# One more transposing transfer, three more masks by ScalarE's copy and a new order in a kernel of attention and feed-forward

## The chip, the cores and the metric

The kernel runs on one core of one Trainium2 chip. A core has five engines: TensorE (PE in the profile, with PEld for its weight loads), VectorE (DVE), ScalarE (ACT), GpSimd (POOL) and SyncE (SP). The metric is device microseconds of one execution. Each text below speaks of "steps" by the names that the kernel gives them.

## The reference

The input is r, k, v, w of shape (4, 8, 768, 48) (batch, heads, time, width), u of shape (8, 48), and four matrices. First comes a recurrence over time for each batch and head, then a feed-forward block on the 3072 tokens.

```
for t in range(S):
    cur = einsum('bhd,bhe->bhde', u * k[t], v[t])
    y[t] = einsum('bhd,bhde->bhe', r[t], state + cur)
    state = w[t][..., None] * state + einsum('bhd,bhe->bhde', k[t], v[t])
x = y transposed and reshaped to (3072, 384)
out = ((x @ w1) * (x @ w2)) @ w3 @ w_out      # 384 -> 1024 -> 1024 -> 384
```

## The kernel before

Time is cut into six chunks of 128 steps. The work is 13 **units**: a unit is one chunk c of one or two batches (`UNITS[t] = (c, b0, nb)`). Units 0 and 1 are the first chunk of batches 0 and 1 alone; every other unit has two batches. The recurrence inside a chunk becomes matrix products, and the state goes from chunk to chunk.

For each unit t there are these steps:

- **Loads:** win, kin, rin, vin (w, k, r, v), each as one DMA from the queue that the order names.
- **Decay:** ln (logarithm of w, ACT), cs or csT (cumulated sum, PE), ne, e, et, iw, pc (exponentials, ACT).
- **Scaled k and r:** KRk, rw, KRr or KRw (multiplies), then their transposes, by PE (trk, trr, trw with the evictions trke, trre) or by a transposing transfer on SP (dtk, dtr).
- **Diagonal term:** rk, ruk, dg, dv: r times k, times u, summed over the width (L530), times v (L539).
- **Scores:** m_t_b (PE, L551), then the mask. There are two ways. `msk` is one DVE multiply from PSUM (L570). For the pairs (t, b) in POOL_MASK it is `mcp`, a copy to SBUF by ACT (L557), and then `maff` on that copy in SBUF: a DVE multiply by the mask (L563) or a POOL select (L565).
- **y:** ys (state part, L586) and yi (scores by v, L596) add up in PSUM. Then `yb` adds dv on DVE (L614). For the units in Y_PE, `yd` adds dv by two PE matmuls with the identity (L605) and `ybc` copies (L611).
- **Transpose of y:** for the units in DMA_Y two transposing transfers on SP, `dty_t_b` (L623); for others `yt` (PE transposes, L633) and `xT` (copy, L637).
- **State:** kv (PE, L667), T (L674), S (times the decay, L689), Sb (copy to bf16).
- **Feed-forward:** a_t_g and b_t_g (PE, L714: x by w1 and by w2, in groups g of 512 columns), asb (copy of a, L719), abT (DVE product of a and b, L724), o_t_b (PE, L730, by the product w34 of w3 and w_out), osb (copy, L735), st (store on SP, L740).

The product w34 is made once, in eight blocks wt, w3Te, wm (L380), w34e. `uc` and `vc_0` cast u and unit 0's v. `warmB@N` runs N matmuls of zeros into PSUM bank B (L308).

What sets the order is a list written out as text, `ORDER`: each entry is `step@engine`, and the program calls the steps in this list's order. Each engine takes its own instructions in that order, and waits in it. `BANKS` gives every step its PSUM bank and its buffers. Between engines only data and buffers order the work. The loads from POOL's queue and POOL's arithmetic stand in one line; the same holds for the transfers and stores on SP.

```
for e in ORDER.split():
    name, _, eng = e.partition("@")
    if name.startswith("warm"):
        warm(int(name[4:]), int(eng))
        continue
    steps[name](eng)
```

Of the kernel before, what the change touches and what calls it, by code (L numbers as in the profile page):

```python
# [62 lines left out]
table@ACT zeros@DVE padlw@DVE win_0@POOL ones@DVE LT@POOL ln_0@ACT warm0@17 cs_0@PE ne_0@ACT win_1@POOL win_2@POOL
kin_2@POOL padkr@DVE csT_0@PE rin_0@SP padr@DVE I128@POOL rin_2@POOL rin_1@POOL rc_0@ACT trw_0@PE et_0@ACT kin_0@SP
kc_0@DVE KRk_0@DVE ln_1@ACT mask1@DVE warm7@2 csT_1@PE pc_0@ACT rk_0@DVE cs_1@PE ne_1@ACT padet@DVE KRw_0@DVE ln_2@ACT
pc_1@ACT trk_0@PE trke_0@DVE kin_1@POOL warm7@2 m_0_0@PE u@SP csT_2@PE cs_2@PE w3_0@POOL vin_0@SP vc_0@DVE kv_0@PE
mcp_0_0@ACT ne_2@ACT uc@DVE ruk_0@DVE dg_0@DVE S_0@DVE rk_2@DVE mask@POOL vin_2@POOL w2_0@POOL KRk_2@DVE trw_2@PE
et_2@ACT dv_0@DVE KRw_2@DVE trk_2@PE trke_2@ACT KRk_1@DVE warm7@5 m_2_0@PE maff_0_0@DVE yi_0_0@PE yd_0@PE ruk_2@DVE
wt_0_0@PE wt_0_1@PE dg_2@DVE et_1@ACT wt_1_0@PE pc_2@ACT mcp_2_0@ACT maff_2_0@DVE trk_1@PE trke_1@DVE w1_1@POOL
vin_1@POOL m_2_1@PE trw_1@PE w2_1@POOL w1_0@POOL kv_2@PE wt_1_1@PE w3Te_0@ACT ybc_0@ACT w3Te_1@ACT win_3@POOL yt_0@PE  # L70
msk_2_1@DVE yi_2_0@PE yi_2_1@PE dv_2@POOL yd_2@PE ybc_2@ACT KRw_1@DVE m_1_0@PE xT_0@DVE rk_1@DVE wo@POOL ruk_1@POOL
# [718 lines left out]
```

## Time and profile before

| | before |
|---|---|
| median of 3 runs | 164.85 us (164.43 to 165.8) |
| the profiled execution: its time | 164.84 us |
| the profiled execution: its span (first to last instruction) | 163.1 us |
| granted TensorE clock | 1.00 |
| PE busy | 154.6 us, 1922 matmuls |
| PE weight loads | 117.4 us |
| DVE busy | 125.2 us, 202 instructions |
| ACT busy | 100.5 us, 166 instructions |
| POOL busy | 97.8 us, 90 instructions |

How to read the rows of the profile: a row of a timeline has start, duration, engine, line of the kernel, operation, output and inputs with their shape, the count of instructions merged in it, and in brackets the idle time before it with what ended that. A row of the windows has, for a stretch of the span, its length, then busy time and count of PE, PEld, DVE, ACT and POOL, the granted clock, the share of the DMA engines and GB/s. A row of the groups has busy time and mean duration in ns, then the idle time in front and what ended it. Rows of the chain of waits have start, duration and what was waited for. Ends of matmuls are modelled and overlap; their starts are recorded.

### The profile page before, as it was taken

The numbers are of one execution on the slowest core, as the hardware profiler recorded it, in microseconds if no ns is written. First come the engines' busy times: TensorE is split into PE (matmuls) and PEld (weight loads), VectorE is DVE, ScalarE is ACT, GpSimd is POOL, SyncE is SP. The second block draws the span as 40 slices with busy tenths as digits, with TensorE's granted clock in tenths as the row PEclk, the third lists the DMA queues.
The fourth block names the chain that finished last, engine by engine and source line by source line (L and its number), as shares of the span: only waits on it lengthen the run. The fifth ranks groups of instructions, "written<-read, shape, count | busy, mean of one in ns | idle before, by whom it ended". The sixth has DMA issues, their size and how long they took to land.

```text
span 163.1 us, 4587 instructions
## 1 busy us (share of the span) xinstructions
PE 154.6 (95%) x1922; PEld 117.4 (72%) x1922; DVE 125.2 (77%) x202; ACT 100.5 (62%) x166; POOL 97.8 (60%) x90
## 2 busy tenths in 40 slices
...
GB/s 119 216 154 184 195 193 244 207 171 212 238 153 174 164 216 244 124 113 83 148 225 99 175 188 147 169 171 144 186 162 158 158 170 95 87 55 45 55 147 96
DMA packets 98837, 25.63 MB, mean 157 GB/s; under 512 B 90880, under 2 KB 96640, under 8 KB 98816
## 3 DMA queue, kind: packets, MB, share of 16 engines
...
## 4 chain that ended last, share of the span: by engine, by line
PE 65%; DVE 14%; DMA 13%; issue 3%; POOL 2%; ACT 1%; DVEq 0%; POOLq 0%; ACTq 0%
PE banks L714 25%; PE banks L730 16%; DMA wo_bf<-in_moe_w_out_dram 8%; PE banks L380 7%; DMA win<-in_w_dram 5%; PE banks L551 3%; DVE dv L539 3%; DVE yb L614 2%; PE banks L371 2%; PE banks L596 2%; DVE abT L724 2%; PE banks L424 2%; PE banks L512 2%; PE banks L667 2%; DVE Mbf L570 1%
## 5 line engine op out<-in xcount | busy, mean ns | idle before, releaser
L714 PE MATMUL banks<-xT,w_bf 128*128 128x256 bf16 (+1 forms) x624 | 69.2, 264 | 0.7 <-DVE yb L614 0.4
L714 PEld LDWEIGHTS <-w_bf 128*128 128x128 bf16 x624 | 55.3, 98 | 8.2 <-issue 1.0
L719 ACT COPY a_sb<-banks 128x512 f32<-128x512 f32 x48 | 27.9, 589 | 25.8 <-PE banks L714 19.0
L724 DVE TENSOR_TENSOR abT<-a_sb,banks 128x512 bf16<-128x512 f32 x48 | 31.6, 682 | 14.9 <-ACT a_sb L719 7.9
L730 PE MATMUL banks<-w,abT 128*128 128x384 bf16 x192 | 33.8, 326 | 0.0
L730 PEld LDWEIGHTS <-abT 128*128 128x128 bf16 x192 | 18.2, 98 | 10.9
L570 DVE TENSOR_TENSOR Mbf<-banks,mask 128x1024 bf16<-128x1024 f32 x15 | 18.1, 1220 | 2.1 <-PE banks L551 2.1
L335 POOL DMA_DIRECT2D win<-in_w_dram x13 | 14.8, 1143 | 5.3 <-ACT NEt L441 3.2
L735 ACT COPY osb<-banks 128x384 f32<-128x384 f32 x21 | 10.0, 482 | 12.8 <-PE banks L730 12.8
L408 ACT ACTIVATE lw<-win 128x768 bf16<-128x768 f32 (+1 forms) x13 | 10.4, 796 | 8.5 <-DMA win<-in_w_dram 8.5
L530 DVE TENSOR_REDUCE dg<-ruk 128x16 f32<-128x768 bf16 (+1 forms) x13 | 11.5, 886 | 0.8 <-POOL ruk L524 0.7
L565 POOL TENSOR_SCALAR_AFFINE_SELECT Mbf<-Mbf 128x1024 bf16<-128x1024 bf16 x5 | 5.5, 1090 | 11.0 <-ACT Mbf L557 11.0
L380 PE MATMUL banks<-wo_bf,w3T 128*128 128x384 bf16 x64 | 11.6, 326 | 0.1
L335 POOL DMA_DIRECT2D kin<-in_k_dram x8 | 9.1, 1133 | 4.1 <-DMA win<-in_w_dram 2.8
L614 DVE TENSOR_TENSOR yb<-banks,dv 128x768 bf16<-128x768 f32 (+1 forms) x11 | 10.1, 919 | 1.8 <-PE banks L596 1.3
L441 ACT ACTIVATE NEt<-banks 128x768 bf16<-128x768 f32 (+1 forms) x13 | 9.9, 764 | 1.5 <-PE banks L424 1.1
L308 PE MATMUL banks<-zeros 128*128 128x512 bf16 x28 | 9.4, 488 | 1.3 <-DVE zeros L249 1.3
L335 POOL DMA_DIRECT2D rin<-in_r_dram x8 | 9.0, 1124 | 2.1 <-DMA w_bf<-in_moe_w_dram 1.5
L557 ACT CAST Mbf<-banks 128x1024 bf16<-128x1024 f32 x9 | 9.0, 1011 | 0.6 <-PE banks L551 0.5
L335 POOL DMA_DIRECT2D vin<-in_v_dram x8 | 9.2, 1148 | 0.2
L524 POOL TENSOR_TENSOR ruk<-rk,u_bc 128x768 bf16<-128x768 bf16 (+1 forms) x4 | 5.8, 1450 | 5.7 <-DVE rk L520 5.7
L380 PEld LDWEIGHTS <-w3T 128*128 128x128 bf16 x64 | 5.8, 98 | 3.6 <-DMA wo_bf<-in_moe_w_out_dram 0.2
(100 smaller groups left out, 244.9 us busy)
## 6 DMA issues: line engine op xcount, KB each, us to landing
...
wo_bf<-in_moe_w_out_dram POOLq DMA_DIRECT2D x1, 768.0 KB, 13.1
```

What stands on the lines that cost most here:

```text
L335: QUEUE[eng].dma_start(dst, src)
L380: nc.tensor.matmul(one(f"wm{fi}")[:, :DM], lhsT=w3T[fi % 2][:, gi, :], rhs=wo_bf[:, gi, :], start=(gi == 0), stop=(gi == FI - 1))
L408: nc.scalar.activation(LW[:, :, :D], ww, Act.Ln)
L441: nc.scalar.activation(N_.rearrange("t (b h) d -> t b (h d)", b=nb), cs_view(), Act.Exp, scale=-1.0)
L530: nc.vector.reduce_sum(dgs, ruks, axis=AX.X)
L570: nc.vector.tensor_mul(Mbf[bank[f"M{t}_{b}"]], mview(), mask.rearrange("s (j q) t -> s j q t", j=2))
L614: nc.vector.tensor_add(ybs.rearrange("t b (q e d) -> t e (b q) d", e=2, d=D), yview().rearrange("t e (x d) -> t e x d", d=D), dvs.rearrang ...
L714: nc.tensor.matmul(o[:, f, :], lhsT=wt[:, di, fi * P:(fi + 1) * P], rhs=x[:, di, :T], start=(di == 0), stop=(di == DI - 1))
L719: copier(eng)(a_sb[bank[f"sa{t}_{g}"]], one(f"a{t}_{g}"))
L724: nc.vector.tensor_mul(ab[:, g * per:(g + 1) * per, :T], sa.rearrange("p (f t) -> p f t", t=T), one(f"b{t}_{g}").rearrange("p (f t) -> p f ...
L730: nc.tensor.matmul(one(f"o{t}_{b}")[:, :DM], lhsT=ab[:, fi, b * C:(b + 1) * C], rhs=w34[:, fi, :], start=(fi == 0), stop=(fi == FI - 1))
L735: copier(eng)(osb[bank[f"so{t}_{b}"]], one(f"o{t}_{b}")[:, :DM])
```

## The change

Three tables of settings change, and the two texts BANKS and ORDER are replaced as a whole. The functions stay as they are.

```diff
-DMA_Y = {4, 9, 10, 11, 12}
+DMA_Y = {4, 6, 9, 10, 11, 12}
-POOL_MASK = {(0, 0), (2, 0), (5, 0), (6, 1), (7, 1), (9, 0), (10, 0), (11, 1), (12, 1)}
-Y_PE = {0, 2}
+POOL_MASK = {(0, 0), (2, 0), (3, 0), (5, 0), (6, 1), (7, 1), (9, 0), (10, 0), (10, 1), (11, 0), (11, 1), (12, 1)}
+Y_PE = {0}
```

- Unit 6's y is transposed by two transfers on SP (dty_6_0, dty_6_1) in place of yt_6 (PE) and xT_6 (DVE).
- The masks (3,0), (10,1) and (11,0) are done by copy and maff in place of msk.
- Unit 2's dv is added by yb_2 on DVE in place of yd_2 (PE) and ybc_2 (ACT).
- win_9 and win_12 are issued by SP in place of POOL: win_9 after dty_4_1 and before dtr_7, win_12 after dtr_8.
- Steps that change engine: from DVE to POOL KRk_11, S_8, dv_11, maff_2_0, maff_12_1, rk_1, ruk_7, ruk_11, rw_8, uc, vc_0; from POOL to DVE KRk_8, KRr_8, maff_6_1, maff_10_0, rk_12, ruk_1, ruk_8, rw_11; from ACT to DVE osb_3_1, 4_0, 5_0, 6_0, 8_1, 11_0, 11_1, trke_3, 4, 5, Sb_6, rc_0, w34e_1, w34e_5, w3Te_1; from DVE to ACT osb_4_1, Sb_0, xT_0, w34e_0, w3Te_2, w3Te_4. New: maff_3_0 and maff_10_1 on DVE, maff_11_0 on POOL.
- The matmuls of zeros at the start: 17, 2, 2, 5, 2 before; 17, 5, 2, 3, 2, 3 after.

The order around the places that the text below speaks of, cut from the list:

```diff
 # before: the start, up to the first feed-forward block of unit 0
-... w3_0@POOL ... mask@POOL vin_2@POOL w2_0@POOL ... KRw_2@DVE ... w1_1@POOL vin_1@POOL ... w2_1@POOL w1_0@POOL ...
-... win_3@POOL yt_0@PE msk_2_1@DVE yi_2_0@PE yi_2_1@PE dv_2@POOL yd_2@PE ybc_2@ACT KRw_1@DVE m_1_0@PE xT_0@DVE rk_1@DVE wo@POOL
-ruk_1@POOL b_0_0@PE yt_2@PE warm5@2 a_0_1@PE ...
 # after
+... uc@POOL w3_0@POOL ... vin_2@POOL vin_0@SP vc_0@POOL ... mask@POOL w2_0@POOL ... w1_1@POOL ... w2_1@POOL vin_1@POOL ...
+... KRw_2@DVE ... w1_0@POOL ... maff_2_0@POOL ... KRk_1@DVE ... dv_0@DVE ... rk_2@DVE ruk_2@DVE dg_2@DVE ... trke_1@DVE ...
+... msk_2_1@DVE KRw_1@DVE ... S_2@DVE yi_2_0@PE yi_2_1@PE m_1_0@PE dv_2@POOL yb_2@DVE ... b_0_0@PE yt_2@PE ... warm7@3
+a_0_1@PE ... win_3@POOL b_2_0@PE wo@POOL rk_1@POOL ...
 # before: units 6 to 8
-... KRr_7@DVE dtr_7@SP S_6@DVE ne_8@ACT xT_5@ACT KRk_8@POOL ... yb_6@DVE ... yt_6@PE ... rw_8@DVE KRr_8@POOL ...
 # after
+... yb_6@DVE ... dty_6_0@SP a_5_0@PE ruk_7@POOL rin_9@POOL ... T_7@DVE ... S_6@DVE trk_7@PE rw_8@POOL KRr_8@DVE ... S_7@POOL ...
+... cs_10@PE ... dtk_8@SP rin_10@POOL dtr_8@SP b_6_0@PE win_12@SP ... KRk_9@POOL ... S_8@POOL ... rw_9@DVE KRr_9@POOL ...
 # after: unit 10
+... ruk_11@POOL ... KRk_11@POOL dtk_11@SP m_10_1@PE ys_10@PE m_10_0@PE dg_10@DVE mcp_10_1@ACT maff_10_1@DVE mcp_10_0@ACT KRr_11@DVE
+dtr_11@SP maff_10_0@DVE kv_10@PE KRk_12@DVE ... rw_12@DVE KRr_12@POOL ...
 # before: units 11 and 12
-... dg_11@DVE dv_11@DVE ... yb_11@DVE ... maff_12_1@DVE ... S_10@POOL ... msk_12_0@DVE rk_12@POOL ruk_12@DVE ...
 # after
+... maff_11_1@POOL ... dg_11@DVE ... maff_11_0@POOL ... S_9@POOL ys_11@PE dv_11@POOL S_10@POOL yi_11_0@PE yi_11_1@PE o_9_0@PE
+yb_11@DVE ... maff_12_1@POOL ...
```

More of the change, by code (lines that the diff above doesn't have):

```diff
@@ L61 @@
 """
 ORDER = """
[L63 to L71, printed above, removed]
-b_0_0@PE yt_2@PE warm5@2 a_0_1@PE asb_0_1@ACT msk_1_0@DVE xT_2@DVE b_2_0@PE S_2@DVE yi_1_0@PE a_2_2@PE dg_1@DVE
@@ L98 @@
-abT_4_2@DVE rw_8@DVE KRr_8@POOL trke_7@ACT ruk_7@DVE Sb_6@ACT kv_7@PE kv_8@PE T_8@DVE xT_6@DVE Sb_5@ACT T_7@DVE
-b_5_0@PE abT_5_0@DVE a_5_2@PE asb_5_3@ACT asb_5_2@ACT b_5_2@PE abT_5_2@DVE o_4_0@PE m_7_0@PE S_8@DVE ys_7@PE rk_8@DVE
-asb_5_1@ACT m_7_1@PE msk_7_0@DVE o_4_1@PE b_5_1@PE ln_9@ACT ruk_8@POOL dg_8@DVE osb_4_0@ACT st_4_0@SP ln_10@ACT
-mcp_7_1@ACT maff_7_1@POOL iw_9@ACT a_6_1@PE asb_6_1@ACT abT_5_1@DVE cs_10@PE ne_10@ACT e_10@ACT S_7@POOL dg_7@DVE
-osb_4_1@DVE st_2_0@SP b_6_1@PE dtr_8@SP pc_10@ACT b_6_2@PE b_5_3@PE win_12@POOL a_6_2@PE yi_7_0@PE yi_7_1@PE
@@ L128 @@
-osb_11_1@ACT st_11_1@SP o_11_0@PE osb_11_0@ACT abT_12_2@DVE st_11_0@SP abT_12_0@DVE abT_12_1@DVE o_12_0@PE o_12_1@PE
-osb_12_0@ACT o_10_1@PE st_12_0@SP osb_12_1@ACT st_12_1@SP osb_10_1@ACT st_10_1@SP
+table@ACT zeros@DVE ones@DVE padet@DVE kin_0@SP win_0@POOL ln_0@ACT LT@POOL padr@DVE padkr@DVE win_1@POOL win_2@POOL
+kin_2@POOL I128@POOL kc_0@DVE padlw@DVE warm0@17 cs_0@PE csT_0@PE et_0@ACT rin_0@SP rin_2@POOL rc_0@DVE trw_0@PE
+KRw_0@DVE ne_0@ACT KRk_0@DVE warm6@5 trk_0@PE ln_1@ACT kin_1@POOL rin_1@POOL ln_2@ACT u@SP uc@POOL w3_0@POOL rk_0@DVE
@@ new lines @@
+ruk_0@DVE trke_0@DVE warm0@2 m_0_0@PE mcp_0_0@ACT dg_0@DVE warm3@3 cs_2@PE cs_1@PE vin_2@POOL vin_0@SP vc_0@POOL
+pc_0@ACT kv_0@PE csT_2@PE mask1@DVE S_0@DVE trw_2@PE mask@POOL w2_0@POOL ne_2@ACT w1_1@POOL KRk_2@DVE trk_2@PE
+w2_1@POOL vin_1@POOL maff_0_0@DVE et_2@ACT KRw_2@DVE trw_1@PE ne_1@ACT w1_0@POOL pc_2@ACT trke_2@ACT warm7@2 m_2_0@PE
+yi_0_0@PE mcp_2_0@ACT maff_2_0@POOL KRk_1@DVE csT_1@PE et_1@ACT dv_0@DVE trk_1@PE yd_0@PE rk_2@DVE ruk_2@DVE dg_2@DVE
+wt_0_0@PE wt_0_1@PE trke_1@DVE pc_1@ACT ybc_0@ACT m_2_1@PE w3Te_0@ACT kv_2@PE yt_0@PE msk_2_1@DVE KRw_1@DVE wt_1_0@PE
@@ new lines @@
+S_2@DVE yi_2_0@PE yi_2_1@PE m_1_0@PE dv_2@POOL yb_2@DVE wt_1_1@PE xT_0@ACT b_0_0@PE yt_2@PE w3Te_1@DVE warm7@3
+a_0_1@PE xT_2@DVE b_2_1@PE a_2_3@PE a_2_2@PE asb_2_2@ACT msk_1_0@DVE asb_2_3@ACT win_3@POOL b_2_0@PE wo@POOL rk_1@POOL
+ruk_1@DVE dg_1@DVE dv_1@DVE yi_1_0@PE yb_1@DVE b_2_3@PE abT_2_3@DVE b_2_2@PE abT_2_2@DVE asb_0_1@ACT ln_3@ACT b_0_1@PE
+abT_0_1@DVE a_0_0@PE asb_0_0@ACT yt_1@PE xT_1@DVE a_2_0@PE kv_1@PE asb_2_0@ACT S_1@DVE Sb_1@DVE abT_0_0@DVE a_1_1@PE
+asb_1_1@ACT abT_2_0@DVE b_1_1@PE csT_3@PE et_3@ACT a_2_1@PE asb_2_1@ACT b_1_0@PE a_1_0@PE cs_3@PE abT_1_1@DVE ne_3@ACT
```

146 lines of the change are left out of this document (75 added, 71 removed).

## Prediction, made before the result was known

> **What bounds the kernel now.** I read the page first, then the busy time by stages, then the timelines of single engines where a stage shows TensorE idle.
>
> ```profile
> span 163.1 us, 4587 instructions
> ...
> PE 154.6 (95%) x1922; PEld 117.4 (72%) x1922; DVE 125.2 (77%) x202; ACT 100.5 (62%) x166; POOL 97.8 (60%) x90
> ```
>
> TensorE (PE) is busy 95% of the span, and the next engine, VectorE (DVE), 77%. The windows below cut the span where PE's behaviour changes; the first figure of a row is the length of the window, the second PE's busy time, and DVE is the third engine figure.
>
> ```profile
> 0.00:23.00 23.00, 18.99 (x204) 10.81 (x205) 15.89 (x41) 13.45 (x21) 19.95 (x27) 1.00 1.45 175
> 23.00:79.00 56.00, 55.94 (x777) 44.34 (x775) 46.41 (x74) 40.14 (x66) 38.22 (x33) 1.00 1.78 183
> 79.00:84.30 5.30, 4.82 (x82) 4.01 (x81) 5.30 (x8) 4.24 (x8) 4.66 (x5) 1.00 1.04 174
> 84.30:133.00 48.70, 48.70 (x634) 37.97 (x631) 42.57 (x62) 32.19 (x54) 35.02 (x28) 1.00 1.63 158
> 133.00:141.00 8.00, 7.78 (x100) 6.33 (x97) 7.45 (x9) 2.99 (x7) 0.00 (x0) 1.00 0.63 120
> ```
>
> From 23 to 141 us PE idles in two places only, 79 to 84.3 and 133 to 141, and in the first of them DVE is busy without a break (5.30 of 5.30). The granted clock is 1.00 throughout. So time can come from three sources: less PE work, an earlier start of the dense part at 23 us, and those two gaps. Because matmul ends are modelled, I measure the gaps from start to start.
>
> ```profile
> 79.80 1.47 PE L714 MATMUL banks<-xT,w_bf 128*128 128x256 bf16 x12
> 81.64 0.81 PE L714 MATMUL banks<-xT,w_bf 128*128 128x256 bf16 x6 [0.37 <-DVE yb L614]
> 82.29 0.50 PE L633 MATMUL banks<-I,yb 128*128 128x128 bf16 x6
> 82.91 0.81 PE L714 MATMUL banks<-xT,w_bf 128*128 128x256 bf16 x6
> ...
> 132.17 0.36 PE L586 MATMUL banks<-Sbf,KRT 64*128 64x48 bf16 x16
> 132.38 0.38 PE L551 MATMUL banks<-KRT 64*128 64x128 bf16 x8
> ...
> 134.51 0.37 PE L586 MATMUL banks<-Sbf,KRT 64*128 64x48 bf16 x16
> 135.03 2.78 PE L714 MATMUL banks<-xT,w_bf 128*128 128x256 bf16 x24
> ...
> 138.05 9.57 PE L714 MATMUL banks<-xT,w_bf 128*128 128x256 bf16 x84
> 147.46 0.81 PE L730 MATMUL banks<-w,abT 128*128 128x384 bf16 x4
> ```
>
> Six matmuls of L714 run from 81.64 to 82.29, 0.65 us. Twelve therefore need 1.30 us, but from 79.80 it took 1.84 until the next: 0.54 lost. The six transposes at 82.29 need 0.33 (half as many columns) and took 0.62: 0.29 lost. At 134.51 the sixteen L586 matmuls took 0.52 where those at 132.17 took 0.21: 0.31 lost. The 84 matmuls from 138.05 took 9.41 where 14 times 0.65 is 9.10: 0.31 lost. Together 1.45 us, in two places. Why DVE is late there stands in four rows of DVE and two of POOL (GpSimd):
>
> ```profile
> 77.31 0.55 DVE L689 TENSOR_TENSOR Sst<-Tst,pc 128x384 f32<-128x384 f32 x1
> ...
> 78.25 2.00 DVE L689 TENSOR_TENSOR Sst<-Tst,pc 128x384 f32<-128x384 f32 x1
> ...
> 130.78 3.05 DVE L539 TENSOR_TENSOR dv<-wo_bf,dg 128x768 bf16<-128x768 bf16 x1
> ...
> 138.19 0.96 DVE L539 TENSOR_TENSOR dv<-vin,dg 128x768 bf16<-128x768 bf16 x1
> ...
> 78.08 1.76 POOL L445 TENSOR_TENSOR KR<-w_bf,NEt 128x768 bf16<-128x768 bf16 x1 [1.91 <-ACT NEt L441]
> ...
> 131.37 1.63 POOL L520 TENSOR_TENSOR rk<-rin,kin 128x768 bf16<-128x768 bf16 x1
> ```
>
> The same state multiply (S, L689) takes 0.55 and 2.00 us, the same dv multiply (L539) 0.96 and 3.05. Each long one ends shortly after a POOL multiply that overlaps it: 80.25 against 78.08 + 1.76 = 79.84, and 133.83 against 131.37 + 1.63 = 133.00. So a DVE multiply of two operands in SBUF waits until POOL's is done, 1.45 and 2.09 us here, and everything behind it on DVE waits too: the yb (L614) that feeds PE at 81.64 is named in PE's own row. The Trainium skill, page "SBUF — State Buffer", section "Who interferes with whom", states this as a lock: a VectorE instruction with two SBUF inputs and a GpSimd instruction that reads SBUF exclude each other for a whole instruction. The two rows agree.
>
> **The change part by part.** *The transfer for y of unit 6* removes yt_6, six PE transposes, 0.33 us of PE, and xT_6, a DVE copy. It adds two transposing transfers on SyncE (SP).
>
> ```profile
> L623 SPq DMA_TRANSPOSE xT<-yb x10: 1177/1242/1312, 62.6 to 142.1; - x10
> ...
> DMA to landing us min/median/max: 2.3/4.0/6.7
> ...
> 80.64 0.94 DVE L614 TENSOR_TENSOR yb<-banks,dv 128x768 bf16<-128x768 f32 x1
> ...
> 91.18 0.33 PE banks L424 x2
> ```
>
> yb_6 ends at 81.6 (80.64 + 0.94). The second transfer is issued one issue (1.3) later and lands after 2.3 to 6.7 us: at 89.6 at worst. Its first reader, b_6_0, stands in the new order right behind cs_10, which is the row at 91.18 and ends at 91.5: a cover of 1.9 us even then. Cost nothing; without that cover, what is missing of it. The transposes go from PE: -0.33.
>
> *y of unit 2 on DVE* removes yd_2 (two PE matmuls) and an ACT copy and adds a yb on DVE, 0.96 us. This lies in the start, which is counted as a whole below.
>
> *Loads of w of units 9 and 12 by SP* take two issues from POOL. On SP they stand in front of dtr_7 and of stores; SP waits long there anyway:
>
> ```profile
> SPq L491 <- DVE KR L486: 13.1, 1, 13.1
> ```
>
> That is SP's wait for KRr_7 before dtr_7, 13.1 us, so an issue ahead of it (some 1.2 to 1.3 us by the transfers above) is hidden, as long as KRr_7 doesn't come over 10 us earlier. Both loads have a buffer whose last reader is long done. Nothing.
>
> *Three more masks by ACT's copy* (units 3, 10, 11).
>
> ```profile
> L570 DVE TENSOR_TENSOR Mbf<-banks,mask x15: 1214/1218/1225, 19.2 to 135.5; 128x1024 bf16<-128x1024 f32 x15
> ...
> L557 ACT CAST Mbf<-banks 128x1024 bf16<-128x1024 f32 x9 | 9.0, 1011 | 0.6 <-PE banks L551 0.5
> ...
> L563 DVE TENSOR_TENSOR Mbf<-Mbf,mask 128x1024 bf16<-128x1024 bf16 x4 | 2.7, 682 | 0.0
> ...
> L565 POOL TENSOR_SCALAR_AFFINE_SELECT Mbf<-Mbf 128x1024 bf16<-128x1024 bf16 x5 | 5.5, 1090 | 11.0 <-ACT Mbf L557 11.0
> ```
>
> DVE loses three masks of 1.22; ACT gains three copies of 1.01; of the second steps (maff) DVE gains two net, 2 x 0.68, POOL one, 1.09. For that, six evictions of the output net go from ACT to DVE. DVE's sum thus stays about where it is, 29 us below PE's, and ACT's and POOL's are lower still: no price as a load.
>
> *The order.* Around the first gap, KRk_8 and KRr_8 go from POOL to DVE, so the POOL multiply at 78.08 is gone; around the second, dv_11 goes to POOL and rk_12 to DVE, so the DVE row of 3.05 is gone, and dv_11 becomes a POOL multiply (1.63 in the row above) beside PE's o_9_0 and ys_11. Both waits end. What is late next is yb, still behind its own abT, dg and masks. The gain is bounded by 1.45 (both gaps close) and by nothing. Other POOL multiplies now stand near DVE's: S_6 beside rw_8, KRr_8 ahead of S_7, rw_9 behind KRk_9 and S_8; each can hold DVE for one POOL multiply. I let 0.5 of the 1.45 come back, a choice between 0 and 1.45 nearer the lower end: net -0.95.
>
> *The start.* In the old order DVE runs back to back from KRw_2 (15.30) to the end of msk_2_1.
>
> ```profile
> 15.30 0.69 DVE L470 TENSOR_TENSOR KRT<-banks,ETt 128x1024 bf16<-128x1024 bf16 x1
> ...
> 19.16 1.22 DVE L570 TENSOR_TENSOR Mbf<-banks,mask 128x1024 bf16<-128x1024 f32 x1
> ...
> 22.08 0.51 PE L633 MATMUL banks<-I,yb 128*128 128x128 bf16 x6
> 22.43 0.59 PE L308 MATMUL banks<-zeros 128*128 128x512 bf16 x2
> 22.86 1.38 PE L714 MATMUL banks<-xT,w_bf 128*128 128x128 bf16 x17
> ...
> 12.89 0.77 POOL L346 DMA_DIRECT2D w_bf<-in_moe_w_dram x1
> ...
> DMA to landing us min/median/max: 9.5/10.6/11.7
> ```
>
> That is 5.08 us (to 20.38). In the new order the two maff in it are gone (-1.2, start to start some 0.08 below the duration), and dv_0, rk_2, KRw_1, S_2 (+0.5, 0.5, 0.35, 0.5) and yb_2 (+0.96) stand ahead of yt_2: 6.6 us, so yt_2 at 21.9 instead of 22.08. Then three warm matmuls instead of two (+0.21; two take 0.43 from 22.43 to 22.86): a_0_1 at 22.9, as before. Bounds: the weights' landing, 12.89 + 9.5 = 22.4, allows -0.45; if nothing overlaps on DVE and ACT, yt_2 comes 0.5 later, +0.7 with the warm matmul. I take 0.
>
> **The sum**, against the profiled execution: its time is 164.84 us beside a span of 163.1, 0.01 from the median of 164.85, so it counts as the median. 0 (start) - 0.33 (yt_6) - 0.95 (gaps) = -1.28, hence **163.6 us**. Bounds of the terms: -0.45 - 0.33 - 1.45 = -2.2, and +0.7 - 0.33 + 0 = +0.4.
>
> **The rivals.** *All of it:* nothing comes back in the gaps and the start takes its 0.45: 162.6. For it: PE has nothing else to wait for. Against: the start hangs on two DVE sums of mine.
> *The gaps stay:* DVE is still late there for other reasons (it was busy 7.45 of 8.00 from 133), and only yt_6 goes: 164.5. For it: DVE's load doesn't fall.
> *Loads later:* POOL's uc, vc_0, maff_2_0 and dv_2 now precede the loads win_3 and wo. The chain of waits of before runs over wo:
>
> ```profile
> 20.23 13.12 DMA wo_bf<-in_moe_w_out_dram
> ```
>
> and PE's first w34 block starts at its landing. maff_2_0 (1.09) and the issue of win_3 (0.77 for the issue quoted above, w's is longer) come between, so wo's issue moves by about 2 us; more PE work ahead of that block, one more L714 block (0.65) and the transposes csT_3 (8/6 of 0.33), covers 1.1. If landings follow the issue, the price is 0.9 to 2.0, say 1.5: 165.1. Against: 13.12 us from issue to landing is mostly queue, and the bytes ahead are the same.
> *Slower, by the wait of the 3.05 row, at unit 10:* the mask steps maff_10_0 and maff_10_1 are now DVE multiplies with both operands in SBUF, while the fifteen old masks, with one operand in PSUM, never took over 1.225 us. POOL has ruk_11, KRk_11 and KRr_12 in its order there, the first two back to back. If m_10 is ready before POOL is through, DVE waits up to 3.3 us (two multiplies of the 1.63 row); DVE was idle for one eighth of that stage (42.57 of 48.70 busy), so of some 6 us there 0.7 is cushion and 2.6 goes through yi_10 and abT to PE: 166.2, up to 166.9. It decides itself at the copy mcp_10_1: after KRk_11's end it costs nothing. The rule of the Trainium skill named above gives just this, since by it a mask out of PSUM has one SBUF input and is free while maff is not; the trace bears out the wait but not that it falls here. That the transfer replaces no work is excluded: yt_6 isn't in the order.
>
> **How the numbers follow.** Forecast 0.42 (own range 162.9 to 164.3), all of it 0.20, gaps stay 0.21, loads later 0.07, slower 0.10. The range 162.2 to 165.9 leaves out the slow case and the far end of the fast one. About 1%, 1.65 us, is what a measurement of this kernel tells from no change: below 163.2 lies a quarter of the forecast's case and nearly all of the fast one, 0.30; above 166.5 the upper half of the slow one and some mishap, 0.08; between, 0.62.
>
> **What would show it.** Right: no S or dv on DVE over 1.2 us near units 6 and 11; PE's busy share full in the stretches that were 79 to 84 and 133 to 141; no L633 row for unit 6; a_0_1 near 22.9. Wrong: a long maff or KR row of DVE near unit 10 or 11; the first L380 matmul after 35 us; L714 waiting for the transposing transfer of unit 6.

## The result, and the profile after

The changed kernel takes 166.72 us in the median of 20 runs (164.97 to 223.75) beside 164.53 us for the kernel before on the same chip (20 runs, 164.24 to 166.5): a ratio of 1.0093, 95% interval 1.0063 to 1.0122. It is 0.9% slower where 0.8% faster was forecast. Medians here and below are of all executions, while the ratios leave out those that took over 1.5% more than the fastest of the same kernel, among them the one of 223.75 us at a granted clock of 0.66 and the profiled ones of g2 and k1 below. The profiled execution took 165.71 us, 1.0 us less than the median, beside a span of 164.0 us.

The page of the kernel after, busy time by engine:

```profile
PE 154.7 (94%) x1916; PEld 116.9 (71%) x1918; DVE 126.3 (77%) x207; ACT 96.2 (59%) x159; POOL 98.6 (60%) x92
```

PE has as much to do as before; the span is longer because it idles more. The windows of the kernel after, cut as those of before (length, PE, PEld, DVE, ACT, POOL, granted clock, DMA share, GB/s):

```profile
0.00:23.00 23.00, 19.19 (x207) 11.18 (x210) 16.01 (x40) 11.49 (x19) 21.10 (x28) 1.00 1.41 176
23.00:79.00 56.00, 55.93 (x779) 44.14 (x777) 48.14 (x78) 39.83 (x66) 37.64 (x33) 1.00 1.87 182
79.00:84.30 5.30, 4.07 (x66) 3.46 (x66) 3.23 (x6) 4.68 (x8) 4.46 (x3) 1.00 2.25 123
84.30:133.00 48.70, 48.02 (x603) 36.93 (x599) 44.86 (x66) 30.05 (x48) 31.82 (x26) 1.00 1.68 165
133.00:141.00 8.00, 8.00 (x130) 6.23 (x129) 4.87 (x5) 2.74 (x5) 3.56 (x4) 1.00 0.69 115
```

The gap at 133 to 141 is closed: 8.00 of 8.00, and DVE there fell from 7.45 to 4.87. The gap at 79 to 84.3 is wider, 4.07 busy instead of 4.82, but DVE is no longer the cause: it is busy for 3.23 of 5.30 where it was busy throughout. PE's timeline names what is late now (start, duration, engine, line, operation, count, idle time before and what ended it):

```profile
82.47 0.43 PE L667 MATMUL banks<-wo_bf,KR 128*64 128x48 bf16 x16
84.13 0.43 PE L667 MATMUL banks<-vin,KR 128*64 128x48 bf16 x16 [1.23 <-DMA vin<-in_v_dram]
...
96.45 0.82 PE L714 MATMUL banks<-xT,w_bf 128*128 128x256 bf16 x6 [0.18 <-DVE abT L724]
...
119.14 0.38 PE L551 MATMUL banks<-KRT 64*128 64x128 bf16 x7 [0.32 <-DVE abT L724]
```

kv_7, the product of the load vin_7, waits 1.23 us for that load. POOL's own timeline of the kernel after shows why it comes late, and the DMA view of the stretch 66 to 78 us, before and after, shows what it meets (the first line is the busy tenths of the DMA engines in 40 slices; the last number of an issue row is the median us to landing):

```profile
63.05 3.52 POOL L524 TENSOR_TENSOR ruk<-rk,u_bc 128x768 bf16<-128x768 bf16 x2 [3.08 <-DVE rk L520]
66.52 1.20 POOL L335 DMA_DIRECT2D kin<-in_k_dram  x1
...
73.78 1.16 POOL L335 DMA_DIRECT2D vin<-in_v_dram  x1
```

The kernel before, 66 to 78 us:

```profile
DMA  9999399999999999999999941000199999999999
...
DMA packets 11292, 1.29 MB, mean 107 GB/s; under 512 B 11273, under 2 KB 11273, under 8 KB 11290
...
vin<-in_v_dram POOLq DMA_DIRECT2D x1, 192.0 KB, 4.4
```

The kernel after, 66 to 78 us:

```profile
DMA  9993229999999999999999999999999999969999
...
DMA packets 10903, 1.78 MB, mean 148 GB/s; under 512 B 10764, under 2 KB 10806, under 8 KB 10901
...
win<-in_w_dram SPq DMA_DIRECT2D x1, 384.0 KB, 5.7
...
vin<-in_v_dram POOLq DMA_DIRECT2D x1, 192.0 KB, 10.2
```

Before, the DMA engines run dry for a few slices just as vin_7 is issued, and it lands in 4.4 us. After, win_9 (SP, at 66.8 us), kin_7 (behind two ruk, of which the first waited 3.08 us) and win_10 all fall into the stretch, 1.78 MB instead of 1.29, and vin_7 takes 10.2 us. It goes on like that; the same view of 77 to 100 us, first before, then after:

```profile
DMA  9997592095999999990009989049995699999999
...
q1 hardware_dynamic: 3744, 1.57, 41.0%
...
KRT<-KR SPq DMA_TRANSPOSE x5, 4.3
```

```profile
DMA  9999999990199999299999999999999999998989
...
q1 hardware_dynamic: 6632, 2.16, 66.3%
...
KRT<-KR SPq DMA_TRANSPOSE x4, 8.0
xT<-yb SPq DMA_TRANSPOSE x2, 7.9
```

The transposing transfers of k and r (KRT) land in 8.0 us instead of 4.3. Two smaller losses are in the rows of DVE and POOL of the kernel after:

```profile
94.72 1.09 DVE L694 CAST Sbf<-Sst 128x384 bf16<-128x384 f32 x1
...
115.66 2.83 DVE L478 TENSOR_TENSOR rw<-w_bf,iw 128x768 bf16<-128x768 bf16 x1
...
114.80 1.67 POOL L524 TENSOR_TENSOR ruk<-rk,u_bc 128x768 bf16<-128x768 bf16 x1
116.41 1.65 POOL L445 TENSOR_TENSOR KR<-w_bf,NEt 128x768 bf16<-128x768 bf16 x1
```

rw_11 ends at 118.49, shortly after POOL's two multiplies back to back (118.06). It makes abT and so the scores at 119.14 late. The cast Sb_6 takes 1.09 us and holds the abT that PE waits for at 96.45.

### The profile page after: what moved, and what is told of

It reads as the page before. It is cut to its first block, busy times and chain, and to the rows that moved or that the text cites. A ratio compares the mean times of both kernels' runs of the same rounds, so it can differ in the third digit from the quotient of the medians.

```text
span 164.0 us, 4598 instructions
## 1 busy us (share of the span) xinstructions
PE 154.7 (94%) x1916; PEld 116.9 (71%) x1918; DVE 126.3 (77%) x207; ACT 96.2 (59%) x159; POOL 98.6 (60%) x92
## 4 chain that ended last, share of the span: by engine, by line
PE 48%; DMA 21%; DVE 12%; POOL 8%; issue 6%; ACT 1%; SPq 0%; POOLq 0%; DVEq 0%; ACTq 0%
PE banks L714 20%; PE banks L730 14%; DMA kin<-in_k_dram 8%; DMA vin<-in_v_dram 6%; PE banks L380 5%; DMA win<-in_w_dram 5%; DVE abT L724 3%; DMA out_dram<-osb 2%; PE banks L551 2%; POOL win L335 2%; POOL dv L539 2%; PE banks L596 2%; DVE dg L530 1%; DVE KR L445 1%; PE banks L371 1%
## 5 line engine op out<-in xcount | busy, mean ns | idle before, releaser
L714 PE MATMUL banks<-xT,w_bf 128*128 128x256 bf16 (+1 forms) x624 | 68.4, 264 | 0.2 <-DVE abT L724 0.2
L719 ACT COPY a_sb<-banks 128x512 f32<-128x512 f32 x48 | 27.0, 591 | 30.6 <-PE banks L714 27.0
L730 PE MATMUL banks<-w,abT 128*128 128x384 bf16 x192 | 34.0, 326 | 0.0
L730 PEld LDWEIGHTS <-abT 128*128 128x128 bf16 x192 | 18.2, 98 | 10.9
L335 POOL DMA_DIRECT2D win<-in_w_dram x11 | 12.7, 1158 | 5.2 <-DMA wo_bf<-in_moe_w_out_dram 2.2
L570 DVE TENSOR_TENSOR Mbf<-banks,mask 128x1024 bf16<-128x1024 f32 x12 | 14.4, 1218 | 1.2 <-PE banks L551 0.8
L557 ACT CAST Mbf<-banks 128x1024 bf16<-128x1024 f32 x12 | 11.9, 1013 | 4.2 <-PE banks L551 4.2
L614 DVE TENSOR_TENSOR yb<-banks,dv 128x768 bf16<-128x768 f32 (+1 forms) x12 | 11.0, 920 | 3.7 <-POOL dv L539 2.8
L735 ACT COPY osb<-banks 128x384 f32<-128x384 f32 x15 | 7.1, 481 | 9.0 <-PE banks L730 9.0
L565 POOL TENSOR_SCALAR_AFFINE_SELECT Mbf<-Mbf 128x1024 bf16<-128x1024 bf16 x6 | 6.5, 1088 | 9.0 <-ACT Mbf L557 9.0
L524 POOL TENSOR_TENSOR ruk<-rk,u_bc 128x768 bf16<-128x768 bf16 x4 | 6.8, 1715 | 6.2 <-DVE rk L520 6.2
L551 PE MATMUL banks<-KRT 64*128 64x128 bf16 x192 | 8.5, 217 | 1.1 <-ACT KRT L516 0.4
## 6 DMA issues: line engine op xcount, KB each, us to landing
vin<-in_v_dram POOLq DMA_DIRECT2D x7, 192.0 KB, 10.2
```

The source lines that it names most:

```text
L335: QUEUE[eng].dma_start(dst, src)
L551: nc.tensor.matmul(o[:, e, q, :], lhsT=KRTs[a:a + PAD, 0, b * HP + q, :], rhs=KRTs[a:a + PAD, 1, b * HP + q, :], start=True, stop=True)
L557: copier(eng)(Mbf[bank[f"M{t}_{b}"]], mview())
L570: nc.vector.tensor_mul(Mbf[bank[f"M{t}_{b}"]], mview(), mask.rearrange("s (j q) t -> s j q t", j=2))
L614: nc.vector.tensor_add(ybs.rearrange("t b (q e d) -> t e (b q) d", e=2, d=D), yview().rearrange("t e (x d) -> t e x d", d=D), dvs.rearrang ...
L714: nc.tensor.matmul(o[:, f, :], lhsT=wt[:, di, fi * P:(fi + 1) * P], rhs=x[:, di, :T], start=(di == 0), stop=(di == DI - 1))
```

## The experiments

Theory N at the outset: each new wait in the line costs by itself. Theory D: the transfers as a whole are late, and the waits only show where. The other letters stand in the expectations. All ratios are to the kernel before on the same chip.

**The kernel after once more, and three places mended one by one.** The expectations:

> The changed kernel as it is, for a second profile. Theory N (new waits in line): the same four places show again: kv_7 waits for the load vin_7 (1.2 us), KRr_8 on DVE takes over 1.1 us, Sb_6 on DVE over 1 us, rw_11 on DVE about 2.8 us; ratio to before 1.007 to 1.012. Theory D (the transfers: two more transposing transfers and two loads on SP make every landing late, so the place changes from run to run): the waits for loads differ from the first profile by over 1 us, the DVE rows may stay. Either way about 166.

```diff
 # e1_rw11_early: VectorE's list
-osb_6_0@DVE rk_11@DVE ruk_10@DVE ... yb_9@DVE ... rw_11@DVE
+osb_6_0@DVE rw_11@DVE rk_11@DVE ruk_10@DVE ... yb_9@DVE ...
```

> rw_11 on DVE moved ahead of rk_11, so that POOL's ruk_11 and KRk_11 can no longer stand in front of it. Theory N: the row of 2.83 us goes to about 0.55, m_10 no longer waits, 0.5 to 0.7 us less than the changed kernel in the same job. Theory D: no change (within 0.3).

```diff
 # e2_loads_early: GpSimd's list
-rin_7@POOL ruk_6@POOL ruk_5@POOL kin_7@POOL kin_8@POOL ... win_10@POOL vin_8@POOL vin_7@POOL
+rin_7@POOL kin_7@POOL ruk_6@POOL ruk_5@POOL kin_8@POOL ... vin_7@POOL vin_8@POOL win_10@POOL
```

> kin_7 issued before POOL's ruk_6 and ruk_5, and vin_7 and vin_8 before win_10. Theory N: vin_7 lands at least 2 us earlier, kv_7 no longer waits, 1.0 to 1.4 us less than the changed kernel in the same job. Theory D: the transfers as a whole stay as slow, another load (kin_9, rin_9 or win_10) is late instead and under 0.4 us is won.

The kernel after again: 166.22 us, 1.0084 [1.0047, 1.0121]. With rw_11 early: 165.94 us, 1.0037 [1.0003, 1.0071]. With the loads early: 165.2 us, 0.9995 [0.9965, 1.0025]. So the late loads cost about 0.9%. For the held rw_11 the difference is about 0.5%, but its interval overlaps that of the kernel after, so a cost of it is not shown. The rows confirm that both waits went: no rw on DVE over 0.55 us in the one, and no wait ahead of kv_7 in the other.

```profile
L478 DVE TENSOR_TENSOR rw<-w_bf,iw x3: 545/550/551, 98.8 to 114.3; 128x768 bf16<-128x768 bf16 x3
```

```profile
83.14 0.43 PE L667 MATMUL banks<-wo_bf,KR 128*64 128x48 bf16 x16
83.42 0.41 PE L667 MATMUL banks<-vin,KR 128*64 128x48 bf16 x16
```

**The forecast's own term, alone.** The two waits of DVE for POOL that the forecast counted, taken out of the kernel before:

```diff
 # e3_before_no_waits: the kernel before
-KRk_8@POOL   (behind xT_5)
+KRk_8@DVE    (behind abT_4_2)
-rk_12@POOL
+rk_12@DVE
```

> The kernel before with only its two long DVE rows taken away: KRk_8 from POOL to DVE and rk_12 from POOL to DVE. The prediction's term: both gaps of PE there close in part or whole, 0.7 to 1.45 us faster than before (ratio 0.991 to 0.996), S_6 near 0.55 us and dv_11 under 1.6 us. If DVE is late there for other reasons too: ratio 0.997 to 1.001.

164.83 us, 0.9986 [0.9957, 1.0015], no change clear of noise. The long DVE rows went (S at most 0.93 us, dv of unit 11 at 1.46). kv_8 starts at 82.77 us instead of 83.92, 1.15 us earlier; 0.41 of that was there at 53 us already, ahead of the edit, so the first gap gave 0.74 of its 0.83. At m_9_0 all of it is still there (105.77 against 106.91). Then PE's timeline shows a new wait, for a copy by ACT (osb_5_1) that idles 2.23 us for a buffer: its store, st_3_1, was issued at 101.18 behind two transposing transfers and landed 6.1 us later.

```profile
107.89 1.46 PE L730 MATMUL banks<-w,abT 128*128 128x384 bf16 x8 [0.74 <-ACT osb L735]
```

Behind it o_6_0 is 0.23 us earlier than before, and the last matmuls 0.11.

The second place gave almost nothing. From the sixteen L586 matmuls of ys_12 to the next L730 it takes 12.89 us (134.45 to 147.34) where it took 12.95 (134.51 to 147.46). DVE has rk_12 to do besides, and PE still waits for the yb of unit 12:

```profile
140.14 7.37 PE L714 MATMUL banks<-xT,w_bf 128*128 128x256 bf16 x66 [0.22 <-DVE yb L614]
```

In the kernel after, where dv_11 is POOL's as well, this place is full.

**Idle time and the clock.** In the kernel after run again, kv_7 waited 2.10 us, and the matmuls behind it took longer:

```profile
84.64 0.43 PE L667 MATMUL banks<-vin,KR 128*64 128x48 bf16 x16 [2.10 <-DMA vin<-in_v_dram]
85.01 2.23 PE L714 MATMUL banks<-xT,w_bf 128*128 128x256 bf16 x12
87.04 1.06 PE L512 MATMUL banks<-I,KR 128*128 128x128 bf16 x8
```

A window of one microsecond in the same run:

```profile
86.00:87.00 1.00, 1.00 (x6) 0.71 (x5) 1.00 (x2) 0.00 (x0) 0.82 (x1) 0.50 2.26 140
```

The granted clock (the figure after the engines) is 0.50. To see whether this is what makes the kernel after slow, the idle time was filled:

```diff
 # f1_warm_fill: the kernel after
-kv_8@PE kv_7@PE
+kv_8@PE warm0@5 kv_7@PE
```

> The kernel after with five matmuls of zeros (some 0.22 us each, into the bank that kv_7 then overwrites) put on TensorE between kv_8 and kv_7, where TensorE idles for vin_7 in the kernel after. Theory I (idle time of some 2 us at kv_7 lets the granted clock fall to half for about 3 us, and that is what makes a part of the runs of the kernel after 1.5 us longer): with the idle down to under 1.1 us the clock stays at 1.00 between 85 and 90 us, the fill costs nothing because it lies in the wait, and the median comes to 165.5 (between 165.2 and 165.9), a ratio of about 1.004, with fewer runs over 166.3. Rival J (the lower clock in those runs comes from elsewhere, not from the idle time): ratio stays at 1.008, 166.2 us, and runs over 166.3 stay as frequent.

165.97 us, 1.005 [1.0015, 1.0085]. In its profile the clock is 1.00 at that place and kv_7 waits 0.53 us more after the fill. The ratio is near theory I's 1.004, but the intervals of filled and unfilled overlap: inconclusive on what the clock costs.

**The mended places together.**

```diff
 # f2_loads_and_rw11: both edits above      # f3_and_sb6: besides
                                            -Sb_6@DVE
                                            +Sb_6@ACT
```

> The kernel after with both mended places: kin_7 right behind rin_7 and vin_7, vin_8 ahead of win_10 (alone 0.9995), and rw_11 ahead of rk_11 on VectorE (alone 1.0037 against 1.0084 of the kernel after). Theory N (each place costs by itself, and nothing is given back behind it): the gains add, 0.9995 - 0.0047 = 0.9948, 164.0 us; L478 on VectorE under 0.7 us and no wait for vin at kv_7. Rival G (what is won ahead is given back at the next late thing, as with the kernel before without its two waits): 0.998 to 1.000, 164.6 to 164.9 us.

> As the kernel with both mended places, and the cast Sb_6 from VectorE to ScalarE besides (1.09 us on VectorE in every kernel of this order, next to a DMA issue on GpSimd). Theory N: abT_6_1 and with it b_6_2 come some 0.5 us earlier, 0.9948 - 0.003 = 0.992, 163.5 us. Rival G: no better than without it, 0.995 to 1.000.

165.21 us, 0.999 [0.9956, 1.0023], and 164.83 us, 0.9982 [0.9956, 1.0008]. The gains don't add: rival G, by which what is won is given back at the next late thing. The profiled execution of the second took 165.74 us, 0.9 us more than its median; in it m_9_0 waits for a transfer that landed in 7.8 us:

```profile
107.81 0.62 PE L551 MATMUL banks<-KRT 64*128 64x128 bf16 x16 [1.54 <-DMA KRT<-KR]
```

The same was tried on the kernel before without its two waits, by issuing the store that held it earlier:

```diff
 # f4_before_nw_store: e3_before_no_waits
-st_2_1@SP ... dtk_9@SP ... dtr_9@SP ... st_3_1@SP
+st_2_1@SP st_3_1@SP ... dtk_9@SP ... dtr_9@SP ...
```

> The kernel before without its two GpSimd waits (KRk_8 and rk_12 on VectorE; alone 0.9986), and the store st_3_1 issued by SyncE right behind st_2_1, ahead of dtk_9 and dtr_9, so that the buffer which osb_5_1 needs is free earlier. Theory S (the 1.14 us won at 84 to 107 us were given back because osb_5_1 waited 2.23 us for that store, which held o_6_0 for 0.74 us): the idle time ahead of o_6_0 goes, 0.9 us come through to the end, ratio 0.993, 163.7 us. Rival T (the next late thing takes its place: the dtk_9, dtr_9 behind the store, or a later buffer): 0.997 to 0.999, 164.3 to 164.7 us.

165.78 us, 1.0024 [0.9992, 1.0055]: rival T, by which the next late thing takes the place, at a time above its range. The wait for the buffer is gone and m_9_0 waits instead, as dtk_9 and dtr_9 now land in 7.7 and 8.0 us:

```profile
107.45 0.62 PE L551 MATMUL banks<-KRT 64*128 64x128 bf16 x16 [1.10 <-DMA KRT<-KR]
```

**The parts of the change alone.**

```diff
 # g1_before_y6: the kernel before, y of unit 6 by transfer
-yb_6@DVE ... yt_6@PE ... xT_6@DVE ... osb_4_0@ACT st_4_0@SP ln_10@ACT mcp_7_1@ACT
+yb_6@DVE dty_6_0@SP ... osb_4_0@ACT st_4_0@SP ln_10@ACT dty_6_1@SP mcp_7_1@ACT
 # k2_before_y6_both: the same, both behind yb_6
+yb_6@DVE dty_6_0@SP dty_6_1@SP
 # g2_before_wsp: the kernel before
-win_9@POOL (behind win_7) ... win_12@POOL (behind b_5_3)
+dty_4_1@SP ... win_9@SP ... dty_4_0@SP ... dtk_8@SP win_12@SP
 # k1_w_pool: the kernel after
-win_9@SP ... win_12@SP
+win_9@POOL (behind win_7) ... win_12@POOL (behind rin_10)
```

> The kernel before with one part of the change alone: y of unit 6 by two transposing transfers (dty_6_0 behind yb_6, dty_6_1 ahead of mcp_7_1, both on SyncE), without yt_6 and xT_6. Theory D (the two transposing transfers crowd the DMA engines from 80 to 95 us, so that everything issued there lands later): the landing time of the transposing transfers dtr_8, dtk_8, dtr_7 goes from 3.2 to 4.3 us in the kernel before towards 6 to 8 us, as in the kernel after (7.5 to 8.3 us); the 0.33 us of yt_6 are won on TensorE, and the time is 165.0 us or more, ratio 1.000 to 1.006. Theory P (as the prediction priced it: hidden): landing times stay under 5.5 us, and the time is 0.3 us shorter, ratio 0.998.

> The kernel before with another part alone: w of units 9 and 12 loaded by SyncE (win_9 behind m_6_0, win_12 behind dtk_8) and no longer by GpSimd. Theory L (place of the loads: win_9 now falls into the stretch where vin_7, vin_8 are loaded): vin_7 lands later than the 4.36 us from issue in the kernel before, but well ahead of kv_7, so the time stays, ratio 0.998 to 1.002. Theory D (the DMA engines are what is late): landing times of dtr_8 and dtk_8 rise by 1 us or more and the ratio is 1.002 to 1.006.

> The kernel after with w of units 9 and 12 issued by GpSimd again, at the neighbours of the kernel before (win_9 behind win_7, win_12 ahead of win_11). Theory L (win_9 by SyncE at 66.8 us falls among the loads of unit 7 and makes vin_7 late): vin_7 lands in under 8 us from its issue instead of 10.2, the wait at kv_7 falls under 0.6 us, and the time is 0.5 to 1.2 us less than that of the kernel after, ratio 1.001 to 1.005. Rival O (vin_7 is late only because kin_7 and win_10 stand ahead of it on GpSimd, whoever issues win_9): the wait at kv_7 stays over 1 us, ratio 1.008; if GpSimd's two further issues of 1.2 us hurt, above that.

> The kernel before with y of unit 6 by two transposing transfers alone, both issued right behind yb_6. In g1_before_y6 the second stood behind the store st_4_0 and a_6_1 waited 1.80 us for it. Theory P (the transfers themselves are hidden, as the prediction priced them): no wait for xT at the products of unit 6, landing times of dtr_8 and dtk_8 at 3 to 6 us, and yt_6's 0.33 us are won: ratio 0.997 to 0.999. Theory D (two more transposing transfers make others late): dtk_8, dtr_8, dtk_9 or dtr_9 land 1.5 us later than in the kernel before, and the ratio is 1.002 or more.

g1 took 167.92 us, 1.0107 [1.0075, 1.014], and g2 169.46 us, 1.0202 [1.0151, 1.0253], each ratio from three executions, both worse than any expectation, and both by their place on SP. In g1 the second transfer stood behind the store st_4_0, was issued at 88.87 us, and a_6_1 waited 1.80 us. In g2 the transposing transfer behind win_9 took 5.04 us to issue (1.3 in the kernel before), and the feed-forward of unit 4 waited; SP's and PE's rows:

```profile
63.60 0.50 SPq L335 DMA_DIRECT2D win<-in_w_dram  x1
64.20 5.04 SPq L623 DMA_TRANSPOSE xT<-yb  x1
```

```profile
75.89 0.83 PE L714 MATMUL banks<-xT,w_bf 128*128 128x256 bf16 x6 [3.43 <-DMA xT<-yb]
```

They are measurements of my places, not of the change's. k1 and k2 are cleaner. k2, both transfers side by side: 165.96 us, 1.006 [1.0039, 1.0081]. dtr_8 and dtk_8 landed in 3.3 and 3.2 us, so the two transfers don't crowd the DMA engines, against theory D, and no product waited for them; yet the part costs 0.6%. These rows tell why, SP's of before, SP's of k2, and ACT's of k2:

```profile
79.83 9.23 SPq L740 DMA_DIRECT2D out_dram<-osb  x3
```

```profile
81.26 2.62 SPq L623 DMA_TRANSPOSE xT<-yb  x2
83.99 6.65 SPq L740 DMA_DIRECT2D out_dram<-osb  x3
```

```profile
89.33 0.48 ACT L735 COPY osb<-banks 128x384 f32<-128x384 f32 x1 [2.07 <-DMA out_dram<-osb]
```

The two issues, 2.62 us, and the wait for yb_6 stand ahead of the store st_3_0 on SP, which starts at 83.99 instead of 79.83; osb_4_0 needs its buffer and holds ACT for 2.07 us, and with it the mask of unit 7 and PE (cs_10 waits 0.68 us). And the 0.33 us of yt_6 are not won: in the old order these transposes ran while PE would have waited for a copy by ACT (a_5_1 waits 0.45 us for an asb in k2).

k1, w of units 9 and 12 by POOL again: 165.19 us, 0.9983 [0.9955, 1.0011]: theory L, by which win_9 falls among the loads of unit 7. Its profiled execution took 168.84 us, with a wait of 2.25 us further on, at m_9_0; it is used for vin_7 and kv_7 alone. In the view of 66 to 78 us vin_7 lands in 8.0 us, and kv_7 starts at 83.70 right behind kv_8 at 83.43:

```profile
vin<-in_v_dram POOLq DMA_DIRECT2D x1, 192.0 KB, 8.0
```

This one edit takes the kernel after from 1.0084 to 0.9983, and the two intervals lie apart. It removes the same wait as the order of POOL's loads did (0.9995), so the two are not to be added.

The Trainium skill, page "DMA: Bandwidth & Descriptors", section "Issuing engines are not separate DMA queues", says that DMAs from different engines run on the same 16 DMA engines and that issuing from several saves only the time of issuing. The rows agree: SP's issue of win_9 cost POOL nothing, and with it POOL's vin_7 took 10.2 us to land, without it 8.0.

**Later loads, and y of unit 6 on PE again,** on the kernel with three places mended:

```diff
 # h1_three_later_loads: f3_and_sb6
-dtr_8@SP ... win_12@SP ... kin_11@POOL ... KRk_9@POOL ... dtk_9@SP ... KRr_9@POOL dtr_9@SP
+dtr_8@SP ... KRk_9@POOL ... dtk_9@SP ... KRr_9@POOL kin_11@POOL dtr_9@SP win_12@SP
 # k3_later_loads_store: h1, and
-o_5_1@PE st_2_0@SP
+st_3_1@SP st_2_0@SP     (some 20 us earlier)
 # h2_three_y6_pe: f3_and_sb6
-dty_6_0@SP ... dty_6_1@SP
+a_5_0@PE yt_6@PE ... abT_4_2@DVE xT_6@DVE
```

> The kernel after with the three places mended (loads of unit 7, rw_11, Sb_6 on ScalarE; 0.9982), and kin_11 and win_12 issued only behind dtk_9 and dtr_9. In the kernel with three places mended m_9_0 waited 1.54 us for dtr_9, which landed 7.8 us after its issue, with kin_11 (14.1 us) and win_12 in flight. Theory Q (loads that are needed late stand ahead of it in the DMA queues): dtr_9 lands in under 6.5 us, the 1.5 us at m_9_0 go, ratio 0.990 to 0.994. Theory R (the transfer is late because dtk_9 and dtr_9 are issued late, behind KRk_9, KRr_9 on GpSimd): m_9_0 still waits over 1 us, ratio 0.997 to 1.000.

> The kernel after with the three places mended (0.9982), and y of unit 6 transposed on TensorE again (yt_6 behind a_5_0, xT_6 on VectorE behind abT_4_2), without the two transposing transfers. Theory D: the landing times of dtr_7, dtk_8, dtr_8 fall from 7.4 to 8.8 us to under 6 us, and the wait of m_9_0 for dtr_9 (1.54 us) shrinks below 0.8 us; with 0.33 us more on TensorE the ratio is 0.992 to 0.996. Theory P (dty_6 is hidden and harmless): landing times as they were, 0.33 us more on TensorE, ratio 1.000.

> h1_three_later_loads (1.012) with the store st_2_0 issued behind st_3_1 at 80 us instead of behind o_5_1 at 102 us, so that its buffer is free for osb_5_1. In h1 the transposing transfers of unit 9 landed in 3.6 and 5.0 us and m_9_0 waited for nothing, but ScalarE idled 3.53 us for that buffer and yt_8 2.45 us. Theory S (that buffer is all that was left): the wait of yt_8 goes and the ratio is 0.992 to 0.996. Theory D (the DMA engines are full from 80 to 107 us, and the store's 196 KB only move the wait): dtr_9 or another transfer is waited for again by over 0.8 us, ratio 0.998 to 1.004.

h1: 166.38 us, 1.012 [1.0074, 1.0166]. Theory Q's mechanism held, dtk_9 and dtr_9 landed in 3.6 and 5.0 us and m_9_0 waited for nothing, but the time got worse: st_2_0, now behind win_12 on SP, landed at 109.23, and PE waited for the buffer.

```profile
109.84 0.50 PE L633 MATMUL banks<-I,yb 128*128 128x128 bf16 x6 [2.45 <-ACT osb L735]
```

h2: 164.94 us, 1.0003 [0.9983, 1.0024], no better than with the transfers (0.9982). dtr_7 and dtk_8 landed in 8.0 and 9.9 us, no earlier than with them (8.0 and 8.8): it is not dty_6 that makes these two late. dtr_9 did land earlier, in 5.4 us instead of 7.8, and m_9_0 waits no more, as theory D had it, but PE now waits 0.70 us for xT_6. k3: 164.47 us, 0.9966 [0.994, 0.9992], the best version of all, and faster than the kernel before by 0.3% (by the near end of the interval 0.1%). The wait of yt_8 went, but 0.54 us at b_8_0 came in its place.

**What the transfers cost in all.**

```diff
 # k5_few_loads: f3_and_sb6, in the function that makes the loads
             src = ROW[x][b0:b0 + nb, :, c * C:(c + 1) * C, :].rearrange("b h t d -> t (b h) d")
+            if t >= 10:
+                dst, src = dst[:, :2], src[:, :2]
```

> The kernel after with the three places mended (0.9982), in which the loads of r, k, v, w of units 10 to 12 bring only the first 2 of 16 heads (of both batches), so that most of their bytes are left out while issue, waits and all arithmetic stay; what is computed of those units is not the reference's. Theory D (the amount of DMA work between 85 and 110 us makes the transposing transfers and stores land late, and this takes the gains): dtk_9 and dtr_9 land in under 5 us instead of 8.8 and 7.8, the waits of m_9_0 (1.54 us) and osb_5_1 (2.5 us) go, ratio 0.986 to 0.992. Rival K (the landing times are set by the order in SyncE's queue and by what the issues wait for): landing times and waits stay, ratio 0.996 to 1.000.

163.37 us, 0.9915 [0.9886, 0.9945]: theory D, at the slow end of its range. Windows, and the landing of the transposing transfers and stores from 95 to 108 us:

```profile
84.30:133.00 48.70, 48.70 (x638) 37.82 (x636) 42.05 (x66) 32.31 (x52) 29.83 (x28) 1.00 0.88 122
133.00:141.00 8.00, 8.00 (x97) 6.84 (x96) 5.63 (x7) 2.45 (x6) 1.34 (x2) 1.00 0.38 102
```

```profile
out_dram<-osb SPq DMA_DIRECT2D x3, 192.0 KB, 2.5
KRT<-KR SPq DMA_TRANSPOSE x3, 3.5
```

PE is busy without a break from 84.3 to 141 us. The same order and queues, with an eighth of the bytes in the loads of three units, give what the mended places were expected to give (0.992), and the interval lies below that with all bytes. dtk_9 and dtr_9 land in 3.5 and 3.0 us instead of 8.8 and 7.8, and dtr_9 is issued only 0.40 us earlier. So the transfer work in flight holds the mended kernel back. Two things stay open. Most of these loads also hold POOL for some 0.75 us an issue instead of 1.17, so not all of the gain need come from the landing. And the kernel before was not run with the same bytes left out, so that the transfers take just the gains that the forecast counted is not shown. The output of those three units is not the reference's, so this is a measurement and no version.

**The rule that follows, tried elsewhere.**

```diff
 # m1_k3_w9_pool: k3_later_loads_store
-win_9@SP
+win_9@POOL (behind vin_5)
 # m2_before_later: f4_before_nw_store, GpSimd's list
-win_12@POOL ... rin_10@POOL kin_11@POOL KRk_9@POOL KRr_9@POOL dv_8@POOL vin_9@POOL rin_11@POOL vin_10@POOL
+rin_10@POOL KRk_9@POOL KRr_9@POOL dv_8@POOL win_12@POOL vin_9@POOL vin_10@POOL rin_11@POOL kin_11@POOL
```

> k3_later_loads_store (0.9966) with win_9 issued by GpSimd behind vin_5, at some 59 us, instead of by SyncE at 67 us. Theory D (what lands while nothing else is needed costs nothing): vin_7 and win_10 land in 5 to 8 us instead of 9.0 and 9.6, the transposing transfers of 78 to 88 us in under 7 us, and as none of them was waited for in k3, the time falls by at most 0.3 us: ratio 0.995 to 0.997. Rival O (GpSimd's issue of 1.2 us ahead of dv_4 and ruk_6 delays yb_4 or KRk_6): a wait of 0.5 us or more at 60 to 70 us, ratio 0.999 or more.

> f4_before_nw_store (1.0024: the kernel before without its two GpSimd waits, st_3_1 early) with win_12 issued behind dv_8 and kin_11 and rin_11 behind vin_10 on GpSimd, so that they no longer stand in the DMA engines ahead of dtk_9 and dtr_9. Theory D: dtk_9 and dtr_9 land in under 5.5 us instead of 7.7 and 8.0, the 1.10 us that m_9_0 waited go, and the 1.14 us won at 84 to 107 us come through: ratio 0.992 to 0.996. Rival T (the wait moves on to vin_9, rin_11 or win_12, which now land later): a wait of over 0.8 us at 107 to 120 us, ratio 0.998 to 1.003.

m1: 165.18 us, 1.0003 [0.9965, 1.0041]; vin_7 landed in 7.3 us instead of 9.0, but csT_6 waited 0.46 us at 62.3 us behind a late yb_4. Rival O, though the intervals of m1 and k3 overlap. Two rows of m1 show why yb_4 is late:

```profile
58.55 1.49 POOL L539 TENSOR_TENSOR dv<-vin,dg 128x768 bf16<-128x768 bf16 x1
```

```profile
59.07 1.40 DVE L478 TENSOR_TENSOR rw<-rin,iw 128x768 bf16<-128x768 bf16 x1
```

The issue of win_9 moves dv_4 on POOL from 57.87 to 58.55 us, and rw_5 on DVE, 0.55 us long in k3, ends only behind it: the wait that the prediction started from, made anew by the place of a load.

m2: 165.09 us, 1.0011 [0.9986, 1.0036]. Again the transfers aimed at came early (4.9 and 4.3 us, no wait at m_9_0), and another store's buffer took the place:

```profile
118.94 3.04 PE L714 MATMUL banks<-xT,w_bf 128*128 128x256 bf16 x24 [1.42 <-ACT osb L735]
```

Rival T, at a store and not at the loads that it named.

## Why the prediction was wrong, point by point

- **The gaps, -1.45 won: right for the first place only.** In the kernel after both long DVE rows are gone and the second place is full. Taken away alone, in e3, the first wait gave 0.74 of its 0.83 us, but the second gave 0.06 of its 0.62: there DVE was late for other reasons too, as the rival "the gaps stay" had it.
- **0.5 of it coming back: mis-sized.** It was chosen from other POOL multiplies only. In e3, 1.04 of the 1.15 us came back (1.15 at kv_8, 0.11 at the end), 0.91 of it between m_9_0 and o_6_0, where a buffer waited for its store. The sum had no term for losses of this kind, at transfers and at buffers.
- **w of units 9 and 12 by SP, "Nothing": the step that failed.** It was priced by SP's free time and by the buffers being free. What counted was the stretch of the DMA engines that win_9 fell into, and with it vin_7, for which PE waited 1.23 and 2.10 us in the two profiles of the kernel after. Undone alone, it moves the kernel after by -1.0%, 1.7 us, as much as its whole loss; by the ends of the two intervals the move lies between 0.4 and 1.7%. POOL's order has a part in it, since e2 takes the same wait away and leaves win_9 on SP. Mended in either way the kernel is level with the one before and not 0.8% faster; the rest of the miss is the gain that came back.
- **y of unit 6, "Cost nothing" and -0.33: the cover was right, the price wrong.** The transfers landed at 88.4 and 89.6 us, within the bound, and b_6_0 at 91.45 waited for nothing. There was luck in it: they took 7.9 us to land where at most 6.7 was counted, and were issued some 1.1 us earlier than counted. Alone in the old order the part costs 0.6%, about 1.0 us, because two issues were put ahead of stores on SP, and I asked only who waits for the transfer, not what stands behind it; and the 0.33 us of PE filled a wait. In the mended new order no cost or gain of it is clear of noise (1.0003 without, 0.9982 with).
- **The start, 0: right.** a_0_1 starts at 22.70 us instead of 22.86.
- **Loads later (win_3, wo):** not seen; wo landed at 32.7 us instead of 33.4.
- **The slower rival:** its mechanism came true, behind the two POOL multiplies it named, at rw_11 instead of maff_10 (the longest maff took 0.88 us), at 2.83 us. What it cost is not shown: mended alone it moved the ratio by 0.5% with overlapping intervals, and with the loads mended by nothing (0.9995 and 0.999). It had a chance of 0.10 and named another instruction.
- **Masks by copy, osb to DVE, nothing:** no row speaks against it, no run tested it.

Open: which of win_9 and win_12 carries the cost of w by SP (k1 moves both); whether the kernel before would gain as much as the mended one from fewer bytes; what the clock's drop costs the kernel after in its median; and how much of the difference between m1 and k3 is real.
